# LayerNorm prologue of a fused attention and FFN kernel: root of the variances by a power on GpSimd, table load ahead of two weight loads, a new prologue order and a new order table

## The chip, the core and the metric

The kernel runs on one core of one Trainium2 chip. The metric is the device time of one execution in microseconds; lower is better. The time before is 662.31 us, the median of three runs (662.22 to 662.44).

## The reference

The input x is 2048 tokens of 640 channels. It is normalised without weights, and two branches read the normalised rows: a multi-query attention with 32 heads of 20 channels that share one key and one value head, and a feed-forward block of 1728 hidden channels with a SiLU. Both are added to x.

```python
xn = (x - mean) / sqrt(var + 1e-5)
q = (xn @ wq) in 32 heads of 20; k = xn @ wk; v = xn @ wv
attn = softmax(q k^T * 20**-0.5) v, heads joined, @ wo
ffn = silu(xn @ w1) @ w2
out = x + attn + ffn
```

## The kernel before

**Attention blocks.** Scores are made in blocks of 128 keys by 512 queries of one head: 32 heads, 4 chunks of queries and 16 key tiles give 2048 blocks. A "score step" (`do_S`, matmuls of L1133) makes three blocks side by side, or four, since each uses 32 rows of the array; three or four PSUM banks must be free. Of a step's blocks, ScalarE takes the exponential of most (L1167, two blocks in one 128x1024 instruction, one in 128x512, three in 128x1536), and VectorE makes the others by clamping them into 16-bit integers that are read as bf16 (L1182); GpSimd (L1221) or VectorE (L1215) adds integer constants to these for two correction terms. The product with the values (`do_pv`, L973) goes in groups of up to four matmuls 32 columns wide, which run side by side; a block of ScalarE needs one matmul, one of VectorE three. The other large matmuls on TensorE, `mm4` at L872, are the query and FFN projections (32x512) and the FFN's second matmul with the output projection (32x320), also in groups of four.

**What sets the order.** `Sched` and `Builder.step` plan the whole program in Python when it is built: each engine's instructions are laid in one fixed order, and semaphores make each wait for what it needs. Between two score steps TensorE takes products with the values or pieces of projections; the planner's choice hangs on a table `SEG` of 64 rows with 29 numbers each (thresholds and priorities, one row for each 32 blocks) and on constants such as `FOUR_FROM` (from which step on four blocks may be taken) and `H0_STEP` (from which step on the first FFN jobs may start). The table holds planned costs and thresholds; the chip sees only the order that comes of it. While TensorE would idle early on, the planner inserts matmuls on zeros ("fills", L848, 128 columns by 512).

**The prologue.** x comes in 16 tiles of 128 tokens by DMAs on SP's queue (`load_x`, L1575), x0 to x3, then 80 columns of wq, then x4 to x15, then the rest of wq. ScalarE's queue asks for wk and wv first (L1591), and only then loads its table for exponentials (L1760). Mean and variance of a tile come from VectorE (two L1685 and one L1687) or, for the six tiles in `ACT_STATS`, from two sums on ScalarE (L1670, L1673) and two small VectorE instructions (L1676, L1680). The reciprocal root is made in three batches of tiles, 0 to 3, 4 to 9 and 10 to 15, by a magic-number start and two Newton steps on GpSimd: ten small instructions for a batch (L1734 to L1750), and two more (L1757, L1758) for minus mean times root where GpSimd normalises. Normalising is one instruction for a tile, on VectorE (L1715) or GpSimd (L1711). The normalised tile xn is then transposed into xnT: tiles 0 to 4 and 13 by TensorE (L1809, five matmuls each) with a copy out of PSUM on ScalarE (L1817, tiles in `T_ACT`) or VectorE (L1820); the ten tiles of `DT` by transposing DMAs on SP's queue (L1775), which stand in one order ahead of further loads. `PRO` writes the order of TensorE's prologue jobs by hand: `t` a transposition, `k` the keys of 256 tokens (L1828), `v` the values of 512 (L1851), `p` half of the first four heads' queries (L872, 32x256), `q1` the next four heads' (32x512). The first score step needs p0, p1 and k0; k and v of later tokens are woven between the score steps that follow.

Of the kernel before, what the change touches and what calls it, by code (L numbers as in the profile page):

```python
# [16 lines left out]
P = 128  # L17
D = 640
# [43 lines left out]
H0_STEP = 10  # L62
# [25 lines left out]
FOUR_FROM = 35  # L88
# [7 lines left out]
PV_HOLD = 12  # L96
# [3 lines left out]
DT = (5, 6, 7, 8, 9, 10, 11, 12, 14, 15)  # L100
NORM_P = 0.9
# [13 lines left out]
STD_COST = 7.4  # L115
K1_ENG = "pool"
PV_MIN = 3
PV_GO = 9
PRO = "t0 t2 t1 p0 t3 k0 k1 p1 q1 v0 t4 k2 v1 k3 k4 t13 v2 k5 k6 v3 k7 d0"
ACT_STATS = (1, 4, 6, 12, 14, 15)  # L120
NW_ENG = ("pool", "pool", "pool")
NORM_ENG = ("pool", "dve", "dve", "dve", "pool", "dve", "dve", "dve", "dve", "pool", "dve", "pool")
# [71 lines left out]
)  # L194
BATCHES = ((0, 4), (4, 10), (10, 16))
T_ACT = (0, 2, 6)


class Op:
# [1741 lines left out]
```

## Time and profile before

| what | value |
|---|---|
| median of three runs | 662.31 us |
| the profiled execution's own time | 662.48 us |
| its span, first to last instruction | 660.7 us |
| granted TensorE clock | 1.000 |

The profiled execution is 0.17 us above the median, and its span lies 1.78 us below its own time. In a timeline a row starts with its start and its length in us; "x8" means that so many like instructions in sequence were merged, and a bracket tells the idle time before it and what ended that. The length of a row of matmuls holds the latency of the last one; what a row costs the engine is read from its start to the start of the next.

### The profile page before, as it was taken

Reading aid. Unit: us, or ns where it says so; the run is one execution under the profiler, and the core shown is the slowest. Engines: PE = TensorE matmul, PEld = TensorE weight load, DVE = VectorE, ACT = ScalarE, POOL = GpSimd, SP = SyncE. Lnnn points to the kernel's source line nnn. Section 1 sums busy time; section 2 is a strip of 40 time slices with the busy share of each in tenths; the row PEclk is TensorE's granted clock in tenths of the full one; section 3 lists DMA queues with packets and bytes.
Section 4 is the critical chain, followed back from the end, with each engine's and each line's share of the span. In section 5 each row is a group of like instructions: output and inputs, shape, how many; then the busy total and the mean of one; then the engine's idle time right before and its main releaser. Section 6 shows DMA issues by size and latency. Waiting matters only on the chain.

```text
span 660.7 us, 22924 instructions
## 1 busy us (share of the span) xinstructions
PE 654.3 (99%) x9762; PEld 220.6 (33%) x9764; DVE 601.5 (91%) x1060; ACT 645.8 (98%) x735; POOL 420.3 (64%) x568
## 2 busy tenths in 40 slices
PE   8999999999999999999999999999999999999998
PEld 4432222323333333333333333333332333333334
DVE  7799999899999997999999979999999998999995
ACT  7899999999999999999999999999999999999995
POOL 6646667676776662676666744677666664766673
PEclk9999999999999999999999999999999999999999
DMA  7566300000004200001003210000000310011001
GB/s 212 97 237 195 88 18 11 10 13 13 14 20 72 73 10 10 10 10 18 18 11 57 63 39 10 18 10 8 12 19 10 77 55 25 10 18 34 11 10 42
DMA packets 52058, 27.89 MB, mean 42 GB/s; under 512 B 37910, under 2 KB 51318, under 8 KB 51958
## 3 DMA queue, kind: packets, MB, share of 16 engines
q1 hardware_dynamic: 50502, 26.22, 15.6%
q8 instruction: 78, 1.28, 0.8%
q10 hardware_dynamic: 1456, 0.22, 0.2%
q14 instruction: 22, 0.18, 0.1%
HBM read 11.44 MB, written 2.62 MB: 21 GB/s over the span
## 4 chain that ended last, share of the span: by engine, by line
PE 92%; ACT 3%; DVE 2%; DMA 2%; SPq 1%; issue 0%; DVEq 0%
PE psall L973 34%; PE psall L1133 29%; PE psall L872 27%; ACT sbt L1167 3%; DMA sbt<-sbt 1%; DVE sbt L1685 1%; DMA sbt<-in_A_x_dram 1%; SPq L1575 0%; DVE sbt L1715 0%; PE psall L1828 0%; PE psall L1369 0%; PE psall L1851 0%; ACT sbt L1379 0%; DVE sbt L1467 0%; DVE sbt L1820 0%
## 5 line engine op out<-in xcount | busy, mean ns | idle before, releaser
L1167 ACT ACTIVATE sbt<-psall 128x1024 bf16<-128x1024 f32 (+2 forms) x644 | 609.6, 1068 | 3.5 <-PE psall L1133 2.9
L1221 POOL INT64_ADD sbt<-sbt x491 | 394.1, 815 | 209.1 <-DVE sbt L1182 183.8
L1182 DVE TENSOR_SCALAR sbt<-psall 128x512 int16<-128x512 f32 x739 | 476.4, 684 | 37.1 <-PE psall L1133 27.6
L973 PE MATMUL psall<-sbt 128*32 128x512 bf16 x3526 | 266.7, 383 | 0.0
L1133 PE MATMUL psall<-sbt 32*128 32x512 bf16 x2048 | 243.6, 384 | 0.3 <-ACT sbt L1167 0.2
L872 PE MATMUL psall<-sbt 128*32 128x320 bf16 (+2 forms) x3939 | 218.3, 331 | 0.3 <-DVE sbt L1687 0.3
L1133 PEld LDWEIGHTS psall<-sbt 32*128 32x128 bf16 x2048 | 61.8, 91 | 235.2 <-issue 80.8
L872 PEld LDWEIGHTS psall<-sbt 128*32 128x32 bf16 x3939 | 85.6, 95 | 85.1 <-issue 50.2
L973 PEld LDWEIGHTS psall<-sbt 128*32 128x32 bf16 x3526 | 63.3, 95 | 99.5 <-issue 68.9
L1384 DVE SCALAR_TENSOR_TENSOR sbt<-sbt,psall 128x512 bf16<-128x512 bf16 x54 | 36.7, 682 | 6.5 <-ACT sbt L1379 6.0
L1379 ACT ACTIVATE sbt<-psall 128x512 bf16<-128x512 f32 x54 | 33.6, 629 | 0.4 <-PE psall L872 0.3
L1285 DVE CAST sbt<-psall 128x512 bf16<-128x512 f32 x32 | 21.9, 683 | 0.6 <-PE psall L973 0.4
L1275 DVE TENSOR_TENSOR sbt<-sbt 128x320 bf16<-128x320 bf16 x31 | 15.8, 510 | 0.0
L1448 DVE SCALAR_TENSOR_TENSOR sbt<-psall,sbt 128x320 bf16<-128x320 f32 x28 | 13.5, 484 | 1.6 <-PE psall L872 1.2
L848 PE MATMUL psall<-sbt 128*128 128x512 bf16 (+2 forms) x44 | 12.9, 447 | 1.4 <-DVE sbt L1624 1.2
L1467 DVE SCALAR_TENSOR_TENSOR sbt<-psall,sbt 128x320 bf16<-128x320 f32 x28 | 13.0, 482 | 1.2 <-PE psall L872 1.2
L1336 DVE TENSOR_SCALAR sbt<-psall 128x512 bf16<-128x512 f32 (+1 forms) x19 | 12.9, 678 | 0.1
L1685 DVE BATCH_NORM_STATS2 sbt<-sbt 128x6 f32<-128x320 bf16 x20 | 8.9, 471 | 3.4 <-DMA sbt<-in_A_x_dram 3.4
L1269 DVE RECIPROCAL sbt<-sbt 128x16 f32<-128x16 bf16 x31 | 7.6, 244 | 0.4 <-DMA sbt<-sbt 0.4
L848 PEld LDWEIGHTS psall<-sbt 128*128 128x128 bf16 x46 | 4.8, 112 | 7.5 <-issue 3.3
L1227 POOL TENSOR_TENSOR sbt<-sbt 128x768 int32<-128x768 int32 x4 | 5.9, 1465 | 0.5 <-DVE sbt L1182 0.5
L1464 ACT ACTIVATE sbt<-psall 128x320 bf16<-128x320 f32 x4 | 1.6, 437 | 4.4 <-PE psall L872 4.3
(72 smaller groups left out, 90.8 us busy)
## 6 DMA issues: line engine op xcount, KB each, us to landing
sbt<-in_A_x_dram SPq DMA_DIRECT2D x32, 160.0 KB, 3.7
out_dram<-sbt SPq DMA_DIRECT2D x15, 160.0 KB, 2.0
sbt<-in_B_w_dram SPq DMA_DIRECT2D x5, 432.0 KB, 5.3
sbt<-sbt SPq DMA_DIRECT2D x105, 20.0 KB
sbt<-in_B_w_dram SPq DMA_DIRECT2D x13, 160.0 KB, 3.0
sbt<-sbt SPq DMA_DIRECT2D x1, 1024.0 KB, 6.3
sbt<-sbt SPq DMA_TRANSPOSE x57, 2.5
sbt<-in_A_wo_dram SPq DMA_DIRECT2D x5, 160.0 KB, 3.0
```

What stands on the lines that cost most here:

```text
L848: return pe.matmul(self.bk(b, 0, n), self.zero[:, 0:P], self.zero[:, 0:n], start=True, stop=True)
L872: ins = pe.matmul(self.bk(b, 0, n, r, r + SLOT), w[:, r:r + SLOT], x, start=start, stop=stop, tile_position=(0, r), skip_group_check=True)
L973: ins = pe.matmul(self.bk(ub[k], 0, QW, r, r + SLOT), self.v[:, it.w, it.kt, :], it.x(), start=f, stop=False, tile_position=(0, r), skip_g ...
L1133: ins = pe.matmul(self.bk(bank[x]), self.kT[r:r + SLOT, kk, kt * P:(kt + 1) * P], self.qT[r:r + SLOT, g % 8, (g // 8) % 2, :], start=True, ...
L1167: return a.activation(self.E[:, b0 * QW:(b0 + na) * QW].rearrange("p (b n) -> p b n", n=QW), src, AF.Exp, scale=ACT_SCALE)
L1182: return v.tensor_scalar(self.Z[:, zs, zp * QW:(zp + 1) * QW], self.bk(bb), 0.0, ZMAX, ALU.max, ALU.min)
L1221: sc.new("pool", tp, lambda v, k=k, c=c: v.int64_add(self.Y[:, zs, k, 0:w].bitcast(I64), self.Z[:, zs, 0:w].bitcast(I64), c), zk + [("lib" ...
L1275: op = sc.new(eng, 0.067 + 16 * DH / 960.0, lambda v: v.tensor_tensor(dst, ut[:, :, :, 0:DH], rb, ALU.mult), [key, ("rL", up)], [("o", h0 ...
L1285: sc.new("dve", t_dve_ps(QW), lambda v: v.tensor_copy(self.U[:, up, :], self.bk(ub)), [("B", ub)], [("U", up)], prio=U_PRIO, name=f"Uev{g}")
L1379: sc.new("act", t_act(QW), lambda a: a.activation(t, src, AF.Tanh, scale=0.5), [("B", b)], [("tb", tp)], prio=TH_PRIO, name=f"th{c}_{fk}") ...
L1384: sc.new("dve", t_dve_ps(QW), lambda v: v.scalar_tensor_tensor(out=self.hT[0:rows, fk, :], in0=t, scalar=1.0, in1=src, op0=ALU.add, op1=AL ...
L1685: np_("dve", 0.41, lambda v, hf=hf: v.bn_stats(self.st6[:, n, hf, :], x[:, hf * 320:hf * 320 + 320]), self.xkeys(n), [("st6", n, hf)], pri ...
```

## The change

- **Root.** The Newton chain, its buffer `nb` and the unused path that normalises on ScalarE go. Each batch's root is now two GpSimd instructions, an add of eps and a `tensor_tensor` with `ALU.pow` against a column of -0.5. GpSimd normalises by subtract and multiply, as VectorE does.
- **Batches.** Five in place of three: tiles 0 to 1, 2 to 3, 4 to 7, 8 to 10, 11 to 15.
- **ScalarE's start.** eps is GpSimd's first memset, the table load and the small activation behind it come first, and wk and wv are asked for only when that activation is done.
- **Prologue order.** `PRO`, `ACT_STATS` (five tiles rather than six), `NORM_ENG`, `T_ACT` and `DT` differ: tile 2 is transposed ahead of tile 0, tiles 6 and 8 go through TensorE instead of 4, and nine tiles rather than ten go by DMA; the aggregation of tile 3 follows its second half's statistics at once (`AG_NEXT`).
- **Order table.** All of `SEG`, and `H0_STEP`, `FOUR_FROM`, `PV_HOLD`, `NORM_P`, two priorities.

On GpSimd, behind the constants of the prologue (L1649 and L1645 before are L1654 and L1650 now), stand these rows before. L1780 is a fill of a query buffer, L1734 to L1750 the Newton chain of tiles 0 to 3, a column for each tile:

```order
L1645 TENSOR_TENSOR sbt<-sbt 128x1
L1649 MEMSET sbt 128x16
L1780 TENSOR_SCALAR sbt<-sbt 128x512
L1734 TENSOR_SCALAR sbt<-sbt 128x4
L1735 TENSOR_SCALAR sbt<-sbt 128x4
L1741 TENSOR_TENSOR sbt<-sbt 128x4
L1748 TENSOR_TENSOR sbt<-sbt 128x4
L1749 TENSOR_SCALAR sbt<-sbt 128x4
L1750 TENSOR_TENSOR sbt<-sbt 128x4
```

And these now, where L1720 adds eps, L1722 is the power, and L1744 is the fill of the query buffer:

```order
L1648 TENSOR_SCALAR sbt<-sbt 128x1
L1654 MEMSET sbt 128x16
L1720 TENSOR_SCALAR sbt<-sbt 128x2
L1722 TENSOR_TENSOR sbt<-sbt 128x2
L1650 TENSOR_TENSOR sbt<-sbt 128x1
L1654 MEMSET sbt 128x16
L1744 TENSOR_SCALAR sbt<-sbt 128x512
L1720 TENSOR_SCALAR sbt<-sbt 128x2
L1722 TENSOR_TENSOR sbt<-sbt 128x2
```

The first batch's root has moved ahead of three older instructions, and the second batch's follows them.

On VectorE the first normalisations (L1715 before, L1711 now) stood behind the statistics of tiles 0, 2, 3, 5, 7, 8 and half of 9; the last of these rows are:

```order
L1685 BN_STATS sbt<-sbt 128x6
L1676 SCALAR_TENSOR_TENSOR sbt<-sbt 128x1
L1685 BN_STATS sbt<-sbt 128x6
L1680 TENSOR_SCALAR sbt<-sbt 128x1
L1687 BN_AGGR sbt<-sbt 128x2
L1685 BN_STATS sbt<-sbt 128x6 x2
L1687 BN_AGGR sbt<-sbt 128x2
L1715 TENSOR_SCALAR sbt<-sbt 128x640 x4
```

Now, with L1690 and L1692 for the statistics, they stand behind tiles 0, 1 and 3, tiles 0 and 1 first, and tiles 2 and 3 behind three half-tiles of statistics of x6 and x7:

```order
L1690 BN_STATS sbt<-sbt 128x6 x2
L1692 BN_AGGR sbt<-sbt 128x2
L1681 SCALAR_TENSOR_TENSOR sbt<-sbt 128x1
L1711 TENSOR_SCALAR sbt<-sbt 128x640 x2
L1685 TENSOR_SCALAR sbt<-sbt 128x1
L1690 BN_STATS sbt<-sbt 128x6 x3
L1692 BN_AGGR sbt<-sbt 128x2
L1711 TENSOR_SCALAR sbt<-sbt 128x640 x2
```

Before, all four normalisations followed the statistics of six and a half tiles; now the first two follow those of three, and the other two those of one and a half more.

TensorE's order up to the first score steps was, with L848 the fills, L1809 transpositions, L872 p0, p1 and q1, L1828 k0 and k1:

```order
L848 MATMUL psall<-sbt 128x512 x33
L848 MATMUL psall<-sbt 128x448
L1809 MATMUL psall<-sbt 128x128 x5
L848 MATMUL psall<-sbt 128x512 x2
L1809 MATMUL psall<-sbt 128x128 x10
L848 MATMUL psall<-sbt 128x512
L848 MATMUL psall<-sbt 128x320
L872 MATMUL psall<-sbt 32x256 x20
L1809 MATMUL psall<-sbt 128x128 x5
L1828 MATMUL psall<-sbt 128x256 x5
```

It is now, with L849, L1773, L873 and L1792 in their places:

```order
L849 MATMUL psall<-sbt 128x512 x26
L849 MATMUL psall<-sbt 128x224
L1773 MATMUL psall<-sbt 128x128 x15
L849 MATMUL psall<-sbt 128x512 x4
L873 MATMUL psall<-sbt 32x256 x20
L1773 MATMUL psall<-sbt 128x128 x5
L1792 MATMUL psall<-sbt 128x256 x5
L849 MATMUL psall<-sbt 128x512 x3
L849 MATMUL psall<-sbt 128x288
```

Seven fills less stand ahead of the first transposition, three tiles are transposed in one go, and more fills stand between k0 and k1 (before, one). Behind these rows k1, p1, q1 and two score steps follow in both.

The diff, cut to its core:

```diff
-H0_STEP = 10
+H0_STEP = 20
-FOUR_FROM = 35
+FOUR_FROM = 15
-PV_HOLD = 12
+PV_HOLD = 16
-DT = (5, 6, 7, 8, 9, 10, 11, 12, 14, 15)
-NORM_P = 0.9
+DT = (4, 5, 7, 9, 10, 11, 12, 14, 15)
+NORM_P = 2.5
+POW_COST = 0.6
+AG_NEXT = 3
-PRO = "t0 t2 t1 p0 t3 k0 k1 p1 q1 v0 t4 k2 v1 k3 k4 t13 v2 k5 k6 v3 k7 d0"
-ACT_STATS = (1, 4, 6, 12, 14, 15)
-NW_ENG = ("pool", "pool", "pool")
+PRO = "t2 t0 t1 p0 t3 k0 k1 p1 q1 t6 v0 k2 k3 t8 v1 t13 k4 k5 v2 k6 k7 v3 d0"
+ACT_STATS = (2, 4, 5, 12, 14)
...
-    (8.178, 1.808, 1.279, 0.2, 2, 4, 1, 2.527, 0.05, 0.93, 0.18, 32, 0.3, 0.573, 10, 6, 2, 54, 24, 30, 6, 0, 1, 0, 99, 0, 2, 0, -9),
+    (1.998, 4.046, 0.633, 0.131, 7, 5, 3, 2.06, 0.05, 1.56, 0.03, 37, 0.11, 0.658, 10, 6, 3, 54, 21, 33, 99, 0, 1, 0, 99, 0, 2, 0, 2.539),
...
-BATCHES = ((0, 4), (4, 10), (10, 16))
-T_ACT = (0, 2, 6)
+BATCHES = ((0, 2), (2, 4), (4, 8), (8, 11), (11, 16))
+T_ACT = (2, 3, 4, 7)
...
+        sc.new("pool", 0.1, lambda g: g.memset(self.eps[:, :], EPS), [], [("eps",)], name="pool")
+        sc.new("act", 1.4, lambda ac: ac.activation(self.tmp[:, 1, 0:1], self.eps[:, :], AF.Exp), [("eps",)],
+               [("warm",)], prio=0.0, name="table")
         for src, k, j in ((self.A_wk, "k", 0), (self.A_wv, "v", 1)):
             sv = src.rearrange("(c p) d -> p c d", p=P)
-            load_w("act", k, [lambda q, sv=sv, j=j: q.dma_start(self.kv_st[:, j, :, :], sv)], ("st", k), 25600)
+            load_w("act", k, [lambda q, sv=sv, j=j: q.dma_start(self.kv_st[:, j, :, :], sv)], ("st", k), 25600, (),
+                   [("warm",)], 1.5 + j)
...
-        def newton(a, b_, pr, eng):
...
+        def root(a, b_, pr):
+            ve = self.tmp[:, 0, a:b_]
+            h = self.half[:, :]
+            hb = bass.AP(self.half, h.offset, [list(h.ap[0]), [0, b_ - a]])
+            add = np_("pool", 0.2, lambda g: g.tensor_scalar(ve, self.mv[:, a:b_, 1], EPS, None, ALU.add), mvk(a, b_),
+                      [("va", a)], prio=pr, name="eps")
+            add.then = np_("pool", POW_COST, lambda g: g.tensor_tensor(self.rstd[:, a:b_], ve, hb, ALU.pow),
+                           [("va", a), ("half",)], [("rs", a)], prio=pr, name="root")
+            add.lock = add.then.lock = True
```

More of the change, by code (lines that the diff above doesn't have):

```diff
@@ L118 @@
 PV_GO = 9
-PRO = "t0 t2 t1 p0 t3 k0 k1 p1 q1 v0 t4 k2 v1 k3 k4 t13 v2 k5 k6 v3 k7 d0"
-ACT_STATS = (1, 4, 6, 12, 14, 15)
-NW_ENG = ("pool", "pool", "pool")
-NORM_ENG = ("pool", "dve", "dve", "dve", "pool", "dve", "dve", "dve", "dve", "pool", "dve", "pool")
+PRO = "t2 t0 t1 p0 t3 k0 k1 p1 q1 t6 v0 k2 k3 t8 v1 t13 k4 k5 v2 k6 k7 v3 d0"
+ACT_STATS = (2, 4, 5, 12, 14)
+NORM_ENG = ("dve", "dve", "dve", "dve", "pool", "pool", "dve", "dve", "pool", "dve", "pool", "dve")
 SEGB = 32
@@ L541, in alloc @@
         self.rstd = sb([P, NT], F32)
-        self.nb = sb([P, NT], F32)
         self.ex2 = sb([P, NT], F32)
@@ L549, in alloc @@
         self.eps = sb([P, 1], F32)
+        self.half = sb([P, 1], F32)
         self.cy = sb([P, 2], I32)
@@ L1576, in load_x @@
                         self.xkeys(n)[:2] if n < NT - 1 else self.xkeys(n)[:1], P * D * 2, sem=s_x[n])
-            op.late = 0.1 if n == 0 else 0.3 if n == 1 else 1.2 if n < 13 else 2.2
+            op.late = (0.1, 0.2, 0.4, 0.6)[n] if n < 4 else 1.4 if n < 13 else 2.2
             op.inc_no = 1
@@ L1624, in prologue @@
         np_("dve", 0.3, lambda v: v.memset(self.zero[:, :], 0.0), [], [("zero",)], prio=-1.0, name="zero")
-        pool(0.1, lambda g: g.memset(self.eps[:, :], EPS), [], [("eps",)])
+        pool(0.1, lambda g: g.memset(self.half[:, :], -0.5), [], [("half",)])
         for k in range(2):
@@ L1684, in stats @@
             for hf in range(2):
-                np_("dve", 0.41, lambda v, hf=hf: v.bn_stats(self.st6[:, n, hf, :], x[:, hf * 320:hf * 320 + 320]),
-                    self.xkeys(n), [("st6", n, hf)], prio=prio, name=f"st{n}")
-            np_("dve", 0.10, lambda v: v.bn_aggr(self.mv[:, n, :], self.st6[:, n, :, :]),
-                [("st6", n, 0), ("st6", n, 1)], [("mv", n)], prio=prio - 0.001, name=f"ag{n}")
+                last = np_("dve", 0.41, lambda v, hf=hf: v.bn_stats(self.st6[:, n, hf, :], x[:, hf * 320:hf * 320 + 320]),
+                           self.xkeys(n), [("st6", n, hf)], prio=prio, name=f"st{n}")
+            op = np_("dve", 0.10, lambda v: v.bn_aggr(self.mv[:, n, :], self.st6[:, n, :, :]),
+                     [("st6", n, 0), ("st6", n, 1)], [("mv", n)], prio=prio - 0.001, name=f"ag{n}")
+            if n == AG_NEXT:
+                last.then = op
         def mvk(a, b_):
@@ L1703, in norm @@
         def norm(n, eng, prio, ra):
-            if eng == "act":
-                np_("act", t_act(D) + 0.186, lambda v: v.activation(
-                    xa(n), self.xslot(n), AF.Identity, scale=self.rstd[:, n:n + 1],
-                    bias=self.nb[:, n:n + 1]), self.xkeys(n) + [("nb", n), ("rs", ra)], [("xn", n)],
-                    prio=prio, name=f"norm{n}")
-                return
-            if eng == "pool":
-                np_("pool", 0.85, lambda g: g.tensor_scalar(
-                    xa(n), self.xslot(n), self.rstd[:, n:n + 1], self.nb[:, n:n + 1], ALU.mult, ALU.add),
-                    self.xkeys(n) + [("nb", n), ("rs", ra)], [("xn", n)], prio=prio, name=f"norm{n}").lock = True
-                return
-            op = np_(eng, 0.36, lambda v: v.tensor_scalar(
+            op = np_(eng, 0.36 if eng == "dve" else 0.85, lambda v: v.tensor_scalar(
                 xa(n), self.xslot(n), self.mv[:, n, 0:1], self.rstd[:, n:n + 1], ALU.subtract, ALU.mult),
@@ L1718, in norm @@
             op.lock = True
-            if n == self.batch[n] and n < 4 and self.last_nw.eng == eng:
-                self.last_nw.then = op
-        def newton(a, b_, pr, eng):
-            v_ = self.tmp[:, 0, a:b_]
-            y_ = self.rstd[:, a:b_]
-            w_ = self.tmp[:, 2, a:b_]
-            ch = []
-            def nw(fn, r, w):
-                ch.append(np_(eng, 0.09, fn, r, w, prio=pr, name="nw"))
-                ch[-1].lock = True
-                self.last_nw = ch[-1]
-                if len(ch) > 1:
-                    ch[-2].then = ch[-1]
-            nw(lambda v: v.tensor_scalar(v_, self.mv[:, a:b_, 1], EPS, None, ALU.add), mvk(a, b_), [("va", a)])
-            nw(lambda v: v.tensor_scalar(y_.bitcast(I32), v_.bitcast(I32), -0.5, 1597463007.0, ALU.mult, ALU.add),
-               [("va", a)], [("rs", a)])
-            m_ = self.mv[:, a:b_, 0]
-            rv, rw, rr = [("va", a)], [("w", a)], [("rs", a)]
-            nb = [("nb", n) for n in range(a, b_)]
-            for _ in range(2):
-                nw(lambda v: v.tensor_tensor(w_, y_, y_, ALU.mult), rr, rw)
-                if eng == "dve":
-                    nw(lambda v: v.scalar_tensor_tensor(out=w_, in0=w_, scalar=-0.5, in1=v_, op0=ALU.mult,
-                                                        op1=ALU.mult), rw + rv, rw)
-                    nw(lambda v: v.scalar_tensor_tensor(out=y_, in0=w_, scalar=1.5, in1=y_, op0=ALU.add,
-                                                        op1=ALU.mult), rw + rr, rr)
-                else:
-                    nw(lambda v: v.tensor_tensor(w_, w_, v_, ALU.mult), rw + rv, rw)
-                    nw(lambda v: v.tensor_scalar(w_, w_, -0.5, 1.5, ALU.mult, ALU.add), rw, rw)
-                    nw(lambda v: v.tensor_tensor(y_, w_, y_, ALU.mult), rw + rr, rr)
-            if all(NORM_ENG[n - 4] == "dve" for n in range(max(a, 4), b_)):
-                return
-            if eng == "dve":
-                nw(lambda v: v.scalar_tensor_tensor(out=self.nb[:, a:b_], in0=m_, scalar=-1.0, in1=y_, op0=ALU.mult,
-                                                    op1=ALU.mult), mvk(a, b_) + rr, nb)
-            else:
-                nw(lambda v: v.tensor_tensor(w_, m_, y_, ALU.mult), mvk(a, b_) + rr, rw)
-                nw(lambda v: v.tensor_scalar(self.nb[:, a:b_], w_, -1.0, None, ALU.mult), rw, nb)
@@ L1760, in prologue @@
-        np_("act", 1.4, lambda ac: ac.activation(self.tmp[:, 1, 0:1], self.eps[:, :], AF.Exp), [("eps",)],
-            [("warm",)], prio=0.0, name="table")
+        def root(a, b_, pr):
[7 more added lines that the diff above has]
+            add.lock = add.then.lock = True
@@ L1766, in prologue @@
                 self.batch[n] = a
-            newton(a, b_, 0.001 * i if b_ <= 4 else 0.3, NW_ENG[i])
+            root(a, b_, 0.001 * i if b_ <= 4 else 0.3)
             if b_ <= 4:
@@ L1780, in prologue @@
         pool(0.95, lambda g: g.tensor_scalar(self.qo[:, :], self.zero[:, 0:QW], self.offq[:, :], 1.0, ALU.add, ALU.mult),
-             [("zero",), ("offq",)], [("qo",)])
+             [("zero",), ("offq",)], [("qo",)], 0.5)
         tb = self.qo[:, :]
@@ L1793, in prologue @@
             load_w1()
-        pool(0.4, lambda g: g.memset(self.w2[:, FC, :], 0.0), [], [("w2z",)])
+        pool(0.4, lambda g: g.memset(self.w2[:, FC, :], 0.0), [], [("w2z",)], 0.5)
         def late_loads(key):
```

124 rows, old and new, of the table SEG are left out of this document.

## The prediction

> **What bounds the kernel now.** I read the page first, then the busy times by stretch.
>
> ```profile
> span 660.7 us, 22924 instructions
> PE 654.3 (99%) x9762; PEld 220.6 (33%) x9764; DVE 601.5 (91%) x1060; ACT 645.8 (98%) x735; POOL 420.3 (64%) x568
> PE 92%; ACT 3%; DVE 2%; DMA 2%; SPq 1%; issue 0%; DVEq 0%
> ```
>
> ```profile
> 10.00:15.00 5.00, 4.37 (x54) 2.64 (x54) 5.00 (x20) 3.89 (x10) 1.60 (x8) 1.00 0.71 240
> 30.00:35.00 5.00, 4.70 (x75) 2.48 (x75) 3.88 (x10) 4.45 (x7) 3.95 (x5) 1.00 0.62 164
> 100.00:150.00 50.00, 49.90 (x747) 15.76 (x743) 47.56 (x81) 50.00 (x56) 36.03 (x45) 1.00 0.05 11
> ```
>
> The span is 1.78 us below the execution's own 662.48, and I take that rest as unchanged. The chain of waits (third line) runs 92% on TensorE. But from 10 to 15 us VectorE is busy without a break: early on it is the bound. From about 35 us TensorE and ScalarE are both full, and a busy share cannot tell which of two full engines sets the pace. Starts of rows can. From the timeline:
>
> ```profile
> 38.03 0.39 PE L1133 MATMUL psall<-sbt 32*128 32x512 bf16 x3
> ...
> 38.36 0.61 PE L872 MATMUL psall<-sbt 128*32 128x512 bf16 x8
> ...
> 38.91 0.39 PE L1133 MATMUL psall<-sbt 32*128 32x512 bf16 x3
> ```
>
> ```profile
> 248.44 0.39 PE L1133 MATMUL psall<-sbt 32*128 32x512 bf16 x4
> 248.76 2.13 PE L872 MATMUL psall<-sbt 128*32 128x512 bf16 x36
> 250.82 0.39 PE L1133 MATMUL psall<-sbt 32*128 32x512 bf16 x4
> ```
>
> ```profile
> 304.20 1.14 PE L872 MATMUL psall<-sbt 128*32 128x320 bf16 x28
> 305.27 0.40 PE L1133 MATMUL psall<-sbt 32*128 32x512 bf16 x4
> ```
>
> A score step costs 0.32 to 0.33 whether it makes three blocks or four. A stretch between steps costs 0.55 for two groups of four and 2.06 for nine: (2.06 - 0.55) / 7 = 0.216 a group, and 0.55 - 0.43 = 0.12 for the change of kind. A group of the 320-wide form costs (1.07 - 0.12) / 7 = 0.136. Now every row of the order can be priced, between these two:
>
> ```profile
> 17.76 0.60 PE L1133 MATMUL psall<-sbt 32*128 32x512 bf16 x6
> ```
>
> ```profile
> 649.90 0.39 PE L1133 MATMUL psall<-sbt 32*128 32x512 bf16 x3
> ```
>
> From the first score step to the last are 632.1 us. Counted in the order of before: 615 single score steps at 0.32 or 0.33 and 3 doubles at 0.55 are 200.3; 614 stretches at 0.115 (between 0.11 and 0.12) 70.6; 1248 groups at 0.216 269.6; 577 of the 320 form at 0.136 78.5; keys, values, transpositions and fills about 9. That is 628.0: **TensorE waits for only some 4 us of 632**, about half of them before 35 us, where it waits for transposing DMAs (bracketed):
>
> ```profile
> 22.93 0.50 PE L1851 MATMUL psall<-sbt 128*128 128x20 bf16 x14 [0.28 <-DMA sbt<-sbt]
> ...
> 29.91 0.65 PE L1851 MATMUL psall<-sbt 128*128 128x20 bf16 x20 [0.39 <-DMA sbt<-sbt]
> ```
>
> So the time is the start of the first score step, plus priced work, plus few waits, plus a tail that is the same in both (the same matmuls stand behind the last score step).
>
> **The change, part by part.**
>
> *The new order of the main part.* Counted the same way, the order of now has 615 single steps (197 of four blocks, before 186) and one double, 604 stretches, 1255 groups and the same 577. That is 2 x 0.55 less, 10 x 0.115 less, 7 x 0.216 more, one transposition more and fills about the same: -1.1 - 1.15 + 1.5 + 0.3 = **-0.45 us**. Does another full engine take that back?
>
> ```profile
> 639.29 12.60 ACT L1167 ACTIVATE sbt<-psall 128x1024 bf16<-128x1024 f32 x14
> ...
> 642.10 5.86 DVE L1182 TENSOR_SCALAR sbt<-psall 128x512 int16<-128x512 f32 x9 [0.20 <-PE psall L1133]
> ```
>
> ScalarE makes 1300 blocks rather than 1309, nine less at 12.60 / 28 = 0.45, so 4 us less; VectorE makes nine more at 0.65, 6 us on an engine that was busy 601.5 of 660.7. Neither becomes the bound by its total. Waits in the new order are bounded from both sides: all 4 us may vanish, or as many may come on top. I keep 4.
>
> *The root.* The chain of before, first and last rows, and GpSimd's dearest and nearest two-input rows:
>
> ```profile
> 6.36 0.69 POOL L1780 TENSOR_SCALAR sbt<-sbt 128x512 bf16<-128x512 bf16 x1
> ...
> 7.97 0.26 POOL L1734 TENSOR_SCALAR sbt<-sbt 128x4 f32<-128x4 f32 x1 [0.93 <-DVE sbt L1687]
> ...
> 8.88 0.20 POOL L1748 TENSOR_TENSOR sbt<-sbt 128x4 f32<-128x4 f32 x1
> ...
> 10.55 0.20 POOL L1750 TENSOR_TENSOR sbt<-sbt 128x4 f32<-128x4 f32 x1
> ```
>
> ```profile
> 29.75 1.47 POOL L1227 TENSOR_TENSOR sbt<-sbt 128x768 int32<-128x768 int32 x1
> ```
>
> Ten instructions took 7.97 to 10.75, 2.8 us. Now there are two: 0.28 for the add and d for the power, which no row shows. I bound d between 0.20 (L1748, a tensor_tensor of four columns) and 1.47 (L1227, the dearest), and take 0.2, since its shape is nearest. The covers: the first root stands on GpSimd three rows ahead of L1744, which began at 6.36 as L1780, so its power starts at about 6.3, and tiles 0 and 1 are normalised as soon as VectorE comes to them. That is near 7.0: VectorE first does the statistics of x0, x1 and x3, 1.0 us each, and then waits for ScalarE's two sums of x2, which was there by 5.08:
>
> ```profile
> 1.80 1.28 ACT L1760 ACT_TABLE_LOAD   x1 [1.80 <-issue]
> ...
> 5.08 0.89 DVE L1685 BATCH_NORM_STATS2 sbt<-sbt 128x6 f32<-128x320 bf16 x2 [0.66 <-DMA sbt<-in_A_x_dram]
> ```
>
> The second root waits for the small instruction behind these two normalisations (7.0 + 2 x 0.35 + 0.15 = 7.85) and for L1744; with the add its power ends at about 8.2 + d. That is needed only when VectorE has done the statistics of x6, which land at 8.13 (ScalarE's sum of x6 starts then):
>
> ```profile
> 8.13 0.74 ACT L1670 ACTIVATE sbt<-sbt 128x640 bf16<-128x640 bf16 x1
> ...
> 11.00 1.46 DVE L1715 TENSOR_SCALAR sbt<-sbt 128x640 bf16<-128x640 bf16 x4
> 11.45 0.45 PE L1809 MATMUL psall<-sbt 128*128 128x128 bf16 x5 [0.23 <-DVE sbt L1715]
> ...
> 13.59 0.62 PE L872 MATMUL psall<-sbt 128*32 128x256 bf16 x16 [0.34 <-DVE sbt L1687]
> ...
> 16.52 1.51 DVE L1715 TENSOR_SCALAR sbt<-sbt 128x640 bf16<-128x640 bf16 x4
> ...
> 16.99 15.69 SPq L1775 DMA_TRANSPOSE sbt<-sbt  x10
> ```
>
> ```profile
> 11.08 1.38 DVE sbt L1715 x4
> ...
> 13.04 0.40 DVE sbt L1820
> ...
> 13.56 1.14 DVE sbt L1685 x3
> 14.70 0.11 DVE sbt L1687
> ```
>
> Three half-tiles at 0.38 and an aggregation of 0.11 (the chain's own rows) put the normalisation of tile 2 at 8.13 + 1.25 = 9.4; it was 11.7 before. The power has a cover of 9.4 - 8.4 = 1 us at d = 0.2. As d delays both roots, the cover is gone at d = 0.9, and from there each 0.1 costs 0.2.
>
> What if GpSimd must first load code for the power? It did so for the 64-bit add:
>
> ```profile
> 46.95 0.18 POOL L1242 INT64_ADD sbt<-sbt  x1 [8.49 <-issue]
> ```
>
> In the built order an instruction of its own stands ahead of that add, and another ahead of the way back; none stands ahead of L1722. I take it at 0 and keep 8.49 for a rival. The Trainium skill, GPSIMD Engine Reference, section 2.1 Instruction dispatch, says that the first call of a freshly loaded kernel pays about 6 us for its code, with no instruction in the profile. L1242's idle time agrees in kind, but is 2.5 us longer. If the power counted as such a kernel, the sum by the page's figure, an estimate, would be near 666 rather than 660.7.
>
> *From there to the first score step.* TensorE's fills do not hold it: 13 were done by 6.27, and the 13.4 left cost 4.48 / 21 = 0.213 each, to 9.2.
>
> ```profile
> 6.27 4.48 PEld L848 LDWEIGHTS psall<-sbt 128*128 128x128 bf16 x21 [0.28 <-issue]
> ```
>
> Transpositions start at about 9.9 (0.45 behind the normalisation, as 11.45 behind 11.00) and last 0.3 a tile, to 10.75. VectorE copies tiles 0 and 1 (0.40 each) from 10.75, to 11.6, so p0 starts at 11.75 against 13.59 before. Then both orders are the same but for the fills. From p0 to the first score step were 4.17 us; 3.6 fills in place of one add 0.5. So the first score step comes at 11.75 + 4.65 = 16.4, against 17.76: **-1.35 us**. VectorE has two more half-tiles of statistics and one more copy to do, 1.2 us; before it idled 3.4 us for tiles of x, all of it ahead of 9 us:
>
> ```profile
> L1685 DVE BATCH_NORM_STATS2 sbt<-sbt 128x6 f32<-128x320 bf16 x20 | 8.9, 471 | 3.4 <-DMA sbt<-in_A_x_dram 3.4
> ```
>
> That covers them, and the normalisation of tiles 4 to 7 ends at about 16.6 rather than 18.0, the rows in between at the same prices. The transposing DMAs follow it (from 16.99 before), so they too come 1.4 us earlier, and TensorE's waits for them keep their distance from the start: 0.
>
> *The table load* (1.28 us, the row above) and the activation behind it end before x2 is there, which is now ScalarE's first statistic: 0. wk and wv are asked for 1.5 us later; k0 and v0 need them past 12 us, so 6 us of statistics and normalising hide that. Were the cover gone, they would cost 1.5.
>
> **Sum.** -1.35 - 0.45 = -1.8 on the profiled execution's 662.48: 660.7. It was 0.17 above the median, so the median should be near 660.5. About 0.2%, 1.3 us, is what a measurement here can tell from no change.
>
> **The rivals.**
>
> *A, forecast, 660.5* (659.3 to 661.8), 0.60.
>
> *B, the start is earlier and the main part gives it back* (about 662.0), 0.22. The new order is packed for four-block steps, which hold four banks until exponentials of 0.9 have run; 1.5 us more waiting eats the gain. For it: ScalarE is at 98%, and the waits of before are as few as they can hardly be. Against: ScalarE's own work falls by 4 us.
>
> *C, the waits go too* (about 658.5), 0.10: the transposing DMAs of later tiles start 1.4 to 2 us earlier while there is one less of them, and the 2 us of waits before 35 us vanish.
>
> *D, the power is dear, slower* (664 to 668), 0.08. The place is the first two roots on GpSimd. The gain of 1.8 is spent at d = 0.9 + 0.9 = 1.8; at d = 1.47 two thirds of it are. At worst the power first needs other code, 8.49 us as L1242: tile 2's normalisation then comes 7.5 later, and the sum is 668. For it: no row shows a power. Against: the missing instruction ahead of it, and a cover of 1 us.
>
> **How the numbers follow.** The range takes in B, C and d up to 1.47, and leaves out D: 658.5 to 662.9. Faster by over 0.2% (below 661.0) are C and nine tenths of A, 0.63; slower by over 0.2% is D, 0.08; the rest, 0.29, lies between.
>
> **What would show it.** The first score step at 16.4, the first transposition at 9.9, tile 2's normalisation near 9.4, L1722 at 0.2 to 0.3 us, the last score step 631.6 us behind the first. A first step at 16.4 with a distance above 632.5 means B; one below 630, C; a first step past 18 with long L1722 rows, D. Wrong would be the sum's first term, if x6's landing does not set tile 2, and the second, if rows no longer follow each other at their price.

## The result, and the profile after

| | before | after |
|---|---|---|
| median of four runs | 662.38 us | 667.66 us |
| profiled execution, its span | 662.48, 660.7 us | 667.23, 665.4 us |
| first score step, last score step | 17.76, 649.90 us | 16.61, 654.56 us |
| granted TensorE clock | 1.000 | 0.995 |

The changed kernel is **0.8% slower**: ratio 1.0079, 95% interval 1.0062 to 1.0096. The forecast was 660.5, 0.3% faster. Executions of some kernels here, of the one before too, fall into two groups some 2 us apart, at granted clocks of 1.000 and about 0.997, and the medians are over both.

The timeline of TensorE in the changed kernel shows the part of the forecast that came true (L1773 are transpositions, L1134 score steps):

```profile
10.14 1.01 PE L1773 MATMUL psall<-sbt 128*128 128x128 bf16 x15 [1.18 <-DVE sbt L1711]
...
16.61 0.60 PE L1134 MATMUL psall<-sbt 32*128 32x512 bf16 x6
...
654.56 0.39 PE L1134 MATMUL psall<-sbt 32*128 32x512 bf16 x3
```

The first score step is 1.15 us earlier. But from the first to the last are 637.95 us, not the 631.6 of the forecast (632.14 before): 5.8 us lost behind the start, and 5.8 - 1.15 = 4.7 is the growth of the span. The same timeline further on, with L1815 the values, L1792 the keys and L974 the products with the values:

```profile
30.67 0.64 PE L1815 MATMUL psall<-sbt 128*128 128x20 bf16 x19
34.46 0.61 PE L1134 MATMUL psall<-sbt 32*128 32x512 bf16 x3 [3.15 <-issue]
...
35.13 1.47 PE L974 MATMUL psall<-sbt 128*32 128x512 bf16 x12
36.53 0.61 PE L1134 MATMUL psall<-sbt 32*128 32x512 bf16 x3
...
39.63 0.39 PE L1134 MATMUL psall<-sbt 32*128 32x512 bf16 x3
```

TensorE stands still for 3.15 us, and then a score step takes 0.61 instead of 0.39 until 39 us. The bracket says "issue": the profile names no releaser. What stood on GpSimd then, in its timeline (L1711 normalises, L1802 copies keys, L1228 adds constants):

```profile
18.78 5.03 POOL L1711 TENSOR_SCALAR sbt<-sbt 128x640 bf16<-128x640 bf16 x2
23.91 0.93 POOL L1802 TENSOR_SCALAR sbt<-sbt 128x256 bf16<-128x256 bf16 x2
...
25.25 1.18 POOL L1722 TENSOR_TENSOR sbt<-sbt 128x5 f32<-128x5 f32 x1
27.38 4.99 POOL L1711 TENSOR_SCALAR sbt<-sbt 128x640 bf16<-128x640 bf16 x2 [0.95 <-DVE sbt L1711]
32.33 1.47 POOL L1228 TENSOR_TENSOR sbt<-sbt 128x768 int32<-128x768 int32 x1
33.88 0.93 POOL L1802 TENSOR_SCALAR sbt<-sbt 128x256 bf16<-128x256 bf16 x2
```

The first of the two key copies at 33.88 takes half of 0.93 and ends near 34.35; the score step starts 0.1 behind it. Ahead of it in GpSimd's order stand an addition of constants (1.47) and two normalisations of 2.5 us each. GpSimd's groups by form show the same row in both kernels, before and after (busy time, mean ns of one):

```profile
L1711 POOL TENSOR_SCALAR sbt<-sbt 128x640 bf16<-128x640 bf16 x4 | 3.5, 875 | 0.0
```

```profile
L1711 POOL TENSOR_SCALAR sbt<-sbt 128x640 bf16<-128x640 bf16 x4 | 10.0, 2511 | 1.1 <-DVE sbt L1711 0.9
```

Same shape, same type, same count, 2.9 times the duration. What differs in the program is the pair of operations, with the two columns that they read: multiply then add before, subtract then multiply now. The power is dearer than was taken too, 0.74 us for two columns to 1.18 for five. So there are three theories of where the loss comes from. **N**: the normalisation's form. **W**: the power. **O**: the new order has the wait built in.

### The profile page after: what moved, and what is told of

Its sections match the earlier page's. It is cut to its first block, busy times and chain, and to the rows that moved or that the text cites. A ratio compares the mean times of both kernels' runs of the same rounds, so it can differ in the third digit from the quotient of the medians.

```text
span 665.4 us, 22939 instructions
## 1 busy us (share of the span) xinstructions
PE 653.7 (98%) x9782; PEld 222.7 (33%) x9782; DVE 607.4 (91%) x1072; ACT 642.5 (97%) x730; POOL 429.0 (64%) x548
## 4 chain that ended last, share of the span: by engine, by line
PE 82%; ACT 13%; DVE 2%; POOL 1%; issue 1%; DMA 0%; DVEq 0%; POOLq 0%
PE psall L974 30%; PE psall L1134 26%; PE psall L873 25%; ACT sbt L1168 13%; DVE sbt L1711 1%; PE psall L1792 1%; DMA sbt<-sbt 0%; PE psall L1370 0%; DVE sbt L1183 0%; DVE sbt L1690 0%; POOL sbt L1722 0%; DVE sbt L1800 0%; PE psall L849 0%; PE psall L1773 0%; POOL sbt L1652 0%
## 5 line engine op out<-in xcount | busy, mean ns | idle before, releaser
L1222 POOL INT64_ADD sbt<-sbt x496 | 400.2, 820 | 205.1 <-DVE sbt L1183 178.5
L1183 DVE TENSOR_SCALAR sbt<-psall 128x512 int16<-128x512 f32 x748 | 482.0, 683 | 38.7 <-PE psall L1134 25.9
L974 PE MATMUL psall<-sbt 128*32 128x512 bf16 x3544 | 271.5, 384 | 0.0
L1134 PE MATMUL psall<-sbt 32*128 32x512 bf16 x2048 | 242.7, 385 | 4.6 <-issue 3.2
L873 PE MATMUL psall<-sbt 128*32 128x320 bf16 (+2 forms) x3939 | 216.2, 330 | 0.0
L1134 PEld LDWEIGHTS psall<-sbt 32*128 32x128 bf16 x2048 | 61.5, 91 | 239.8 <-issue 96.5
L873 PEld LDWEIGHTS psall<-sbt 128*32 128x32 bf16 x3939 | 86.8, 95 | 82.3 <-issue 49.5
L974 PEld LDWEIGHTS psall<-sbt 128*32 128x32 bf16 x3544 | 63.8, 95 | 100.2 <-issue 67.1
L849 PE MATMUL psall<-sbt 128*128 128x512 bf16 (+5 forms) x44 | 12.2, 423 | 1.2 <-DVE sbt L1629 1.2
L1690 DVE BATCH_NORM_STATS2 sbt<-sbt 128x6 f32<-128x320 bf16 x22 | 9.8, 471 | 2.2 <-DMA sbt<-in_A_x_dram 2.2
L1711 POOL TENSOR_SCALAR sbt<-sbt 128x640 bf16<-128x640 bf16 x4 | 10.0, 2511 | 1.1 <-DVE sbt L1711 0.9
L1792 PE MATMUL psall<-sbt 128*128 128x256 bf16 x40 | 6.4, 296 | 1.2 <-DMA sbt<-sbt 1.0
L849 PEld LDWEIGHTS psall<-sbt 128*128 128x128 bf16 x44 | 4.4, 109 | 7.1 <-issue 3.2
```

The source lines that it names most:

```text
L849: return pe.matmul(self.bk(b, 0, n), self.zero[:, 0:P], self.zero[:, 0:n], start=True, stop=True)
L873: ins = pe.matmul(self.bk(b, 0, n, r, r + SLOT), w[:, r:r + SLOT], x, start=start, stop=stop, tile_position=(0, r), skip_group_check=True)
L974: ins = pe.matmul(self.bk(ub[k], 0, QW, r, r + SLOT), self.v[:, it.w, it.kt, :], it.x(), start=f, stop=False, tile_position=(0, r), skip_g ...
L1134: ins = pe.matmul(self.bk(bank[x]), self.kT[r:r + SLOT, kk, kt * P:(kt + 1) * P], self.qT[r:r + SLOT, g % 8, (g // 8) % 2, :], start=True, ...
L1183: return v.tensor_scalar(self.Z[:, zs, zp * QW:(zp + 1) * QW], self.bk(bb), 0.0, ZMAX, ALU.max, ALU.min)
L1222: sc.new("pool", tp, lambda v, k=k, c=c: v.int64_add(self.Y[:, zs, k, 0:w].bitcast(I64), self.Z[:, zs, 0:w].bitcast(I64), c), zk + [("lib" ...
```

## The experiments

All but after_honest (and the one move in after_dvenorm) keep the order of every engine: rows are put in or replaced behind the planner, so what differs is the row. The ratios are to the kernel before in executions taken together with each experiment, where its median was 662.2 to 662.7.

### The form of the normalisation, in the changed kernel and in the kernel before

after_multadd:

```diff
+  w  = mean * rstd            # two small rows behind each of the last two powers
+  nb = w * -1
-  GpSimd: tensor_scalar(xa, x, mean, rstd, subtract, mult)
+  GpSimd: tensor_scalar(xa, x, rstd, nb, mult, add)
```

> The changed kernel, same order on every engine, but GpSimd normalises its four tiles by multiply and add (rstd and a bias -mean x rstd from two small instructions behind each of the last two powers), as before the change. Theory N (the subtract/multiply form on GpSimd, 2.51 us against 0.875, is what costs): GpSimd rows of the normalisation at 0.88, GpSimd free 6.5 - 0.9 = 5.6 us earlier by 33 us, no wait of 3.15 us at 31.3, granted clock 1.0 from 30 to 40 us, time 661.5 (660.8 to 662.3). Theory W (the power, 0.7 to 1.2 us where 0.2 was taken, is what delays GpSimd): the five powers stay, so the wait stays and the time stays above 666. Theory O (the new order has the wait built in): the order is the same, so the time stays above 666.

Measured: **661.1 us**, ratio to before 0.9979 (0.9969 to 0.9989). GpSimd's timeline of this kernel (L1736 normalises, L1829 copies keys), and TensorE's at the place of the wait (L1157 are score steps):

```profile
26.21 1.74 POOL L1736 TENSOR_SCALAR sbt<-sbt 128x640 bf16<-128x640 bf16 x2 [0.38 <-DVE sbt L1734]
...
29.36 0.48 POOL L1829 TENSOR_SCALAR sbt<-sbt 128x256 bf16<-128x256 bf16 x1
```

```profile
16.61 0.60 PE L1157 MATMUL psall<-sbt 32*128 32x512 bf16 x6
...
29.36 0.64 PE L1842 MATMUL psall<-sbt 128*128 128x20 bf16 x19
29.94 0.39 PE L1157 MATMUL psall<-sbt 32*128 32x512 bf16 x3
...
648.15 0.39 PE L1157 MATMUL psall<-sbt 32*128 32x512 bf16 x3
```

The key copy now ends at 29.84 and the score step follows at 29.94 without a wait. From first to last step are 631.54 us; 631.6 was forecast. N holds: with powers and order in place, one form is worth 6.6 us (667.66 to 661.1). W and O fall as causes of the loss.

before_submult is the opposite edit, the kernel before with subtract and multiply on GpSimd:

```diff
-  GpSimd: tensor_scalar(xa, x, rstd, nb, mult, add)
+  GpSimd: tensor_scalar(xa, x, mean, rstd, subtract, mult)
```

> The kernel before, same order, with one edit: GpSimd normalises its four tiles by subtract and multiply (mean, rstd). Theory N: four rows of 2.5 in place of 0.875, GpSimd 6.5 us later, TensorE waits for it or for the transposing DMAs behind its tiles before 40 us: slower than before by 2 to 6 us, 664.5 to 668. Theories W and O: no power and the old order, so 662.4.

Measured: 667.22 us, ratio 1.0073 (1.0052 to 1.0094). With neither power nor new order, the one edit makes the old kernel as slow as the changed one. Here the profile names the releaser (L1809 is a transposition):

```profile
21.35 0.23 PE L1809 MATMUL psall<-sbt 128*128 128x128 bf16 x1 [1.66 <-POOL sbt L1711]
```

A lower clock is not needed for this loss: two executions with the clock at 1.000 took 667.04 and 667.30 us, and the profiled one, at 0.992, took 667.63.

### Which operation of the pair it is

after_multsub multiplies first and then subtracts (mean times rstd, one small row); after_addmult adds minus the mean and then multiplies:

```diff
+  after_multsub: tensor_scalar(xa, x, rstd, mean * rstd, mult, subtract)
+  after_addmult: tensor_scalar(xa, x, -mean, rstd, add, mult)
```

> As after_multadd, but GpSimd's normalisation is multiply by rstd, then subtract mean x rstd (one small instruction instead of two). If the subtraction is what makes the row dear: 2.5 us a row and a time near 667. If the multiplication as the second operation is dear: 0.88 a row and 660.8 to 661.2.

> As after_multadd, but GpSimd adds -mean and multiplies by rstd (one small instruction in place of two behind each of the last two powers). If the subtraction alone makes the row dear, in either place, and not the place of the multiplication: 0.88 a row, and with 0.2 to 0.3 us less on GpSimd per root a time of 660.6 to 661.1. If a multiplication behind another operation is dear: 2.5 a row and 667.

Measured: after_multsub 667.0 (1.0076, 1.0059 to 1.0093) with 2.50 us a row; after_addmult 661.44 (0.9980, 0.9969 to 0.9990) with 0.87. The subtraction makes the row dear in either place.

gpsimd_prices measures the rows alone, on a dead buffer behind GpSimd's last row:

```diff
+  L535 add, mult   L536 subtract, mult   L537 mult, add   L538 mult, subtract
+  L539 add only    L540 subtract only    L541 mult only   L542 subtract, mult by immediates
+  L543 subtract, mult on 320   L544 mult, add on 320   L545 L546 L547 powers of 1, 8, 16 columns
```

> As after_multadd with 18 rows added on GpSimd behind its last row, on a dead buffer: its time is not to be read, only the rows' durations (128x640 bf16, scalars from a column). Theory S (subtraction is done slowly on GpSimd): add/multiply and multiply/add 0.88, subtract/multiply and multiply/subtract 2.5, subtraction alone 1.5 or more where addition alone is 0.9 or less; 320 columns about half. Powers of 1, 8 and 16 columns at 0.58, 1.63 and 2.8 by the line 0.43 + 0.15 a column.

Its timeline of GpSimd:

```profile
658.57 0.88 POOL L535 TENSOR_SCALAR sbt<-sbt 128x640 bf16<-128x640 bf16 x1
659.54 2.53 POOL L536 TENSOR_SCALAR sbt<-sbt 128x640 bf16<-128x640 bf16 x1
662.17 0.88 POOL L537 TENSOR_SCALAR sbt<-sbt 128x640 bf16<-128x640 bf16 x1
663.14 2.51 POOL L538 TENSOR_SCALAR sbt<-sbt 128x640 bf16<-128x640 bf16 x1
665.75 1.90 POOL L539 TENSOR_SCALAR sbt<-sbt 128x640 bf16<-128x640 bf16 x1
...
671.70 2.36 POOL L542 TENSOR_SCALAR sbt<-sbt 128x640 bf16<-128x640 bf16 x1
674.16 1.43 POOL L543 TENSOR_SCALAR sbt<-sbt 128x320 bf16<-128x320 bf16 x1
675.69 0.60 POOL L544 TENSOR_SCALAR sbt<-sbt 128x320 bf16<-128x320 bf16 x1
676.38 0.60 POOL L545 TENSOR_TENSOR sbt<-sbt 128x1 f32<-128x1 f32 x1
677.06 1.66 POOL L546 TENSOR_TENSOR sbt<-sbt 128x8 f32<-128x8 f32 x1
678.79 2.90 POOL L547 TENSOR_TENSOR sbt<-sbt 128x16 f32<-128x16 f32 x1
```

The four pairs came as expected. The single operations did not: an addition alone costs 1.90 (a subtraction or multiplication alone 1.89), more than twice an addition with a multiplication behind it. So it is not that subtraction is slow; of the eight forms at 640 columns here only add with mult, in either order, is fast. Why, no run here shows. The power's line, 0.43 + 0.15 a column, holds to 16 columns.

### What the wait costs beside its length

after_fill puts matmuls on zeros into the place of the wait and leaves all else:

```diff
   TensorE: values x19
+  TensorE: 14 matmuls on zeros, 128x512, into the bank of the score step that follows
   TensorE: score step
```

> The changed kernel as it is, with 14 more fills of 512 columns (2.98 us at 0.213) on TensorE in the place where it waits 3.15 us for GpSimd's key copies, ahead of the score step at 34.46. The wait itself is as long as before. Theory I (the granted clock falls because TensorE idles for 3 us): clock 1.0 from 30 to 40 us in place of 0.74 and 0.58, and the 2.4 us of rows at 0.61 in place of 0.39 between 34 and 39.5 us go: 665.0 to 665.6 against 667.7. Theory L (the clock falls for another reason, load of all engines or time since the start): it falls all the same, 667.5 to 668.

Measured: 665.14 us, ratio to before 1.0043 (1.0028 to 1.0058). Busy time by stretch (the last three columns are granted clock, DMA share and GB/s) in the changed kernel:

```profile
30.00:35.00 5.00, 1.85 (x29) 0.89 (x27) 1.68 (x4) 2.44 (x4) 4.73 (x4) 0.74 0.31 70
35.00:40.00 5.00, 5.00 (x39) 1.81 (x40) 3.65 (x9) 3.08 (x3) 1.95 (x2) 0.58 0.88 279
```

The same in after_fill, and its timeline (L522 are the added matmuls):

```profile
30.00:35.00 5.00, 4.97 (x48) 2.30 (x50) 1.83 (x5) 2.59 (x5) 4.70 (x4) 1.00 0.32 72
35.00:40.00 5.00, 4.99 (x69) 2.31 (x65) 4.93 (x12) 4.75 (x6) 2.42 (x3) 1.00 0.88 285
```

```profile
31.17 3.18 PE L522 MATMUL psall<-sbt 128*128 128x512 bf16 x14
34.38 0.39 PE L1155 MATMUL psall<-sbt 32*128 32x512 bf16 x3
```

The score step starts where it did (34.38 against 34.46), but the clock stays at 1.00 and the step takes 0.39. Theory I holds: 2.5 us of the loss (667.66 to 665.14; 2.1 by the two spans) was the clock that fell because TensorE stood still. The run shows the releaser too, which the profile did not name: the added matmuls wait for all that the score step waits for except GpSimd, and they began at 31.17, behind the values, so the step's wait was for GpSimd alone.

### The root: what the power is worth, and its cover

after_newton puts the nine small rows of before in place of the power, after_newton_multadd does that and the multiply/add as well, before_power puts the power into the kernel before, and after_multadd_pow2 does the first two powers of after_multadd twice (before_power also has one small memset more, for the column of -0.5):

```diff
-  GpSimd: eps, pow                                  (after_newton, after_newton_multadd)
+  GpSimd: eps, magic start, 2 x (mult, mult, mult-add, mult)
-  GpSimd: eps, magic start, 2 x (mult, mult, mult-add, mult)      (before_power)
+  GpSimd: eps, pow
-  GpSimd: eps, pow            (after_multadd_pow2, tiles 0 to 1 and 2 to 3)
+  GpSimd: eps, pow, pow
```

> The changed kernel, same order, but the root is taken by the nine small instructions of before in place of the power; GpSimd keeps subtract/multiply. Theory N: rows of the normalisation stay at 2.5, the wait near 31.3 us stays, and as a chain of nine rows of 0.2 and their gaps takes some 1.5 us more than a power of 0.7, the first score step is later by 0.5 to 1.5: 668 to 669.5. Theory W: GpSimd is late no more, 662 to 663. Theory O: about 667.7.

> The changed kernel with the root of before (nine small instructions) and GpSimd's multiply/add of before: what is left of the change is the new order and the early table load. Theory O: above 666. Theory N: no long wait, first score step later than the changed kernel's 16.61 by 0.5 to 1.5, time 661.5 to 663.

> The kernel before, same order, with one edit: the root is the power (one row) in place of eight of the small rows; GpSimd's multiply/add stays. Theory R (the first roots set the start, the power shortens it): the first power ends near 9.35 where the chain ended at 10.77, the first transposition comes 1.4 us earlier than 11.45, the first score step at 16.5 to 16.9 instead of 17.76, time 661.2 to 661.6 against 662.4. Theory W (the power does harm): 662.4 or more.

> As after_multadd, with the first two powers done twice (same result, 0.74 more on GpSimd for each). By the prediction's cover (gone at 0.9, then 0.2 us for each 0.1): 1.48 in place of 0.74 costs 1.2 us, 662.3, first score step 17.8. If the cover was gone already at 0.74: 1.6 or more, 662.7 to 663.5. If the roots do not set the start: 661.1.

| kernel | us | ratio to before | first score step |
|---|---|---|---|
| after_newton | 676.19 | 1.0209 (1.0187 to 1.0230) | 22.00 |
| after_newton_multadd | 668.24 | 1.0091 (1.0060 to 1.0123) | 22.21 |
| before_power | 663.15 | 1.0011 (1.0000 to 1.0023) | 17.61 |
| after_multadd_pow2 | 664.48 | 1.0022 (1.0009 to 1.0036) | 18.10 |

W falls again: without the power the kernel is slower, not faster. But all four medians lie outside the ranges given for N, for R and for the two cases of the cover, and they tell where the power pays. In after_newton two chains of 2.7 to 2.8 us stand in series ahead of the first transpositions, where after_multadd has two powers of 0.7, and TensorE runs out of fills (L1802 are transpositions):

```profile
13.47 1.78 PE L1802 MATMUL psall<-sbt 128*128 128x128 bf16 x15 [4.92 <-DVE sbt L1738]
```

The granted clock is then 0.61 and 0.71 in the two stretches between 10 and 20 us, and the first step is 5.4 us late, not the 0.5 to 1.5 expected: 3.3 up to the first transposition (13.47 against 10.14), and 2.1 behind it, where the clock is low. In before_power the same exchange, the other way, gains nothing that can be measured. Its 663.15 lies where W was expected (662.4 or more), but its interval begins at no change, and its first step is 0.15 earlier and not later. Its power (L527) ends at 9.5, but VectorE reaches the normalisations (L1744) only at 10.70, since six half-tiles of statistics stand ahead of them in its order (in the kernel before, at 11.00):

```profile
8.44 1.06 POOL L527 TENSOR_TENSOR sbt<-sbt 128x4 f32<-128x4 f32 x1
```

```profile
9.84 0.83 DVE L1714 BATCH_NORM_STATS2 sbt<-sbt 128x6 f32<-128x320 bf16 x2
10.59 0.19 DVE L1716 BATCH_NORM_AGGREGATE sbt<-sbt 128x2 f32<-128x12 f32 x1
10.70 1.46 DVE L1744 TENSOR_SCALAR sbt<-sbt 128x640 bf16<-128x640 bf16 x4
```

So the earlier start comes from power and prologue order together; neither alone has it. In after_multadd_pow2, two more powers of 0.74 delay the first step by 1.49, one for one: at 0.74 no cover is left. (The profiled execution, from which the 18.10 is read, took 662.86 us; the median is 664.48.)

### Other ways out of the long rows

after_dvenorm gives GpSimd's four tiles to VectorE; after_honest tells the planner the true prices and lets it plan anew:

```diff
+  after_dvenorm: norm8, norm9, norm12, norm14 on VectorE, where GpSimd's began in the plan
-  after_honest: planned 0.85 for a normalisation on GpSimd, 0.6 for a power
+  after_honest: planned 2.5, and 0.43 + 0.15 a column
```

> The changed kernel with GpSimd's four normalisations given to VectorE (subtract/multiply as it does them, 0.38 a row), at the places in VectorE's order where GpSimd's began in the plan; nothing else moves. GpSimd loses 10 us of work before 33 us, VectorE gets 1.5 us where it was busy 4.9 of 5, 4.4 of 5 and 3.9 of 5 us. Theory N (GpSimd's long rows are the loss): the wait of 3.15 us goes, 660.8 to 662. If VectorE is the bound there, TensorE waits for its evictions instead: 662.5 to 664.

> The changed kernel with two numbers of the planner set to what the rows took: 2.5 instead of 0.85 for a normalisation on GpSimd, 0.43 + 0.15 a column instead of 0.6 for the power. The code of the rows is the same, the order is planned anew on every engine. If the loss comes only from the long rows standing where nobody expects them, a plan that knows them has no 3 us wait and lands at 661 to 664; if GpSimd's 10 us cannot be placed before 40 us, 665 to 668.

Measured: after_dvenorm 661.57 (0.9981, 0.9971 to 0.9991), as N says. after_honest **682.62** (1.0299, 1.0279 to 1.0318), far outside both cases. Its wait is gone, but its order is another one through the whole program: it makes the 2048 blocks in 633 score steps (154 of four blocks) where after_multadd makes them in 617 (197 of four), and it has 37 fills 32 columns wide (L840) where that has none. TensorE is busy 670.2 us here and 651.6 there. Why the same table of 64 rows gives so much worse an order with two other prices, no run shows, and so this run says nothing on the long rows. The fastest versions are after_multadd, after_addmult and after_dvenorm, 0.2% below the kernel before and not told apart by their intervals.

## Why the prediction was wrong

**The step that failed** is the one on tiles behind the first four: "The transposing DMAs follow it ..., so they too come 1.4 us earlier, and TensorE's waits for them keep their distance from the start: 0". The DMAs did come earlier (15.78 against 16.99 before), but they were the only wait that this step looked at. It took GpSimd's share of that stretch, with the key copies in GpSimd's order, as unchanged, and there TensorE lost its time. The description of the change says that GpSimd now subtracts and multiplies, but no price was set on it; the row at 875 ns is of another form, and no row of the kernel before shows a subtraction with a multiplication on GpSimd. This was an operation that the trace did not show, and the prediction bounded the power and not this one. With 2.5 us bounded in, 4 x 1.63 = 6.5 us on GpSimd between 19 and 32 us would have been a rival by itself.

**The bound on the waits** ("as many may come on top", 4 us) failed with it. Between after and after_multadd the distance from first to last step differs by 637.95 - 631.54 = 6.4 us. The wait is 3.15 of that, and the low clock 2.1 (665.4 - 663.3, the spans of after and after_fill; 1.9 of it lies between the score steps that start at 34.46 and 39.63). Two smaller waits are longer (L1802 is the key copy): 0.74 is new, and the one for a transposing DMA is 0.96 against 0.67 in after_multadd, 1.03 together.

```profile
20.52 0.71 PE L1792 MATMUL psall<-sbt 128*128 128x256 bf16 x5 [0.96 <-DMA sbt<-sbt]
...
24.44 0.39 PE L1134 MATMUL psall<-sbt 32*128 32x512 bf16 x3 [0.74 <-POOL sbt L1802]
```

That makes 6.3 of the 6.4. In after_fill, which has the long rows too, the same two waits are 0.65 and 1.05, again 1.70 in sum: where the DMA is earlier, the key copy takes up the difference, so these 1.03 us are GpSimd's as well.

**The start** was right in size: first step at 16.61 (forecast 16.4), first transposition at 10.14 (9.9). The missing 0.2 is the power, taken at 0.2 and measured at 0.74. Its cover was said to last to 0.9; VectorE's timeline shows that it was used up:

```profile
7.21 1.21 DVE L1711 TENSOR_SCALAR sbt<-sbt 128x640 bf16<-128x640 bf16 x2 [0.44 <-POOL sbt L1722]
...
8.40 1.26 DVE L1690 BATCH_NORM_STATS2 sbt<-sbt 128x6 f32<-128x320 bf16 x3
9.59 0.18 DVE L1692 BATCH_NORM_AGGREGATE sbt<-sbt 128x2 f32<-128x12 f32 x1
9.69 0.74 DVE L1711 TENSOR_SCALAR sbt<-sbt 128x640 bf16<-128x640 bf16 x2
```

The first normalisation waits for the power, and from there VectorE runs without a break to tile 2 at 9.69: its own row of work sets that place, not the landing of x6. The 8.13 was only an upper bound for that landing: ScalarE's instruction ahead of that row ran from 7.86 to 8.05.

**The main part** came out as counted in steps (418 of three blocks, 197 of four and one double). -0.45 us was forecast, and after_multadd has 631.54 against 632.14 from first to last step, -0.6. That agrees, but executions of one kernel spread by 0.5 us and more, so two profiles do not show a gain of this size. **The table load and the weights** cost nothing: no row of TensorE waits for them.

**The rivals.** By the prediction's own test, an early first step and a distance above 632.5, this was B (the main part gives it back). That test was too coarse: B's mechanism, steps of four blocks that hold banks, is in after_multadd as well, with a distance of 631.54, and the loss lies ahead of 40 us. C (waits vanish) did not happen. D named 664 to 668, and the time lies in it, but its mechanism is refuted: the power costs 0.74 to 1.18, no idle time for code stands ahead of it, so the rule of the Trainium skill, GPSIMD Engine Reference, section 2.1 Instruction dispatch, on a first call's 6 us did not apply to it, and after_multadd keeps all five powers and is 0.2% faster than before. That the sign of D came true is chance.

## What to carry to other kernels

An instruction whose operations change is a new instruction, even if line, shape, type and engine stay: price it or bound it, above all on GpSimd. Follow an engine's order behind the lengthened row, since in the changed kernel the loss came through the key copies queued there; in before_submult a transposition waited for the row's own result. A wait on TensorE costs its length and can cost the clock behind it: look at the durations behind the gap before the sum is closed, and where it can't be removed, fill it.

## What the runs showed of the hardware

- **GpSimd's two-operation rows**, 128x640 bf16: add with mult 0.88, either order; any pair with a subtraction 2.36 to 2.53; one operation alone 1.89 to 1.90. A subtraction is had for 0.88 as the addition of a negated column. At 320 columns 0.60 and 1.43.
- **A power on GpSimd**: 0.43 + 0.15 us a column, f32, 1 to 16 columns.
- **The granted clock falls within or just behind waits of 1.7 to 4.9 us and stays down for whole steps of 3.41 us, in three traces.** TensorE's busy time and clock in the changed kernel, by microsecond (length, busy time and rows, clock, DMA share, GB/s):

```profile
31.00:32.00 1.00, 0.31 (x13) 1.00 0.73 164
32.00:33.00 1.00, 0.00 (x0) 0.69 0.00 0
...
38.00:39.00 1.00, 1.00 (x7) 0.50 0.99 237
39.00:40.00 1.00, 1.00 (x12) 0.90 0.98 397
```

and in before_submult, where the wait was 1.66 us long:

```profile
21.00:22.00 1.00, 0.65 (x4) 0.79 0.52 116
...
31.00:32.00 1.00, 1.00 (x8) 0.59 0.50 111
```

If the clock is 1.0 or 0.5 and nothing between, 0.69 means that it fell at 32.38, and 0.90 that it rose at 39.20: 6.82 us. In before_submult it fell at 21.58 and rose at 31.82: 10.24 us, though TensorE was busy without a break from 25 us on. In after_newton the clock is 0.53 from 11 to 12 us and 0.55 from 17 to 18, so it fell at 11.06 and rose at 17.90: 6.84 us. These are two, three and two times 3.41. The Trainium skill, TensorE: Matmul & The Clock Gate, section What's actually happening, gives a free-running window of 3413 ns, and the trace agrees. Its section HAM oscillation — how this bites in real kernels speaks of idle gaps longer than about 3.4 us as what brings the clock down; here it fell 1.1 us into the wait of 3.15, and in before_submult 0.2 us behind the end of the wait of 1.66, so a gap of half that length was enough. It does not always suffice: in after_multadd_pow2 the clock stayed at 1.00 over a wait of 1.71.
